# First two gate and up steps on raw x, normalised afterwards, in a spectral-filter and feed-forward kernel

## Chip, cores and metric

The kernel runs on one core of one Trainium2 chip. The metric is the device time of one execution in microseconds. Engines: PE is TensorE (matmuls into PSUM), DVE is VectorE, ACT is ScalarE, POOL is GpSimd, SP is the engine that issues most DMA transfers.

## What is computed

With x of shape (2048, 640) in bf16, and w_gate, w_up (640, 1536), w_down (1536, 640):

```python
xn = (x - mean(x)) / sqrt(var(x) + 1e-5)          # along the 640 columns
s  = irfft2(rfft2(xn) * (w_r + 1j * w_i))         # a two-dimensional spectral filter
h  = gelu(xn @ w_gate) * (xn @ w_up)
g  = silu(h @ w_down)
out = x + s * g
```

## The kernel before, in words

The 2048 rows are sixteen **slabs** of 128 rows, n1 = 0 to 15, four slabs to a **group** (512 rows). A slab goes through these steps:

- Its rows are loaded (`load_x`; DMA issues on SP's queue have line L294) and its mean and 1/sigma are found. `stats` does this on DVE (two `bn_stats` of 320 columns, L393, an aggregate, L396, an add, L397) or on ACT (a pass that sums, L400, then a pass that sums squares, L403), and POOL takes the power -0.5 (L416, L417).
- `apply` (L430, DVE) writes the normalised slab.
- For slabs 0 to 3, `turn_pe` transposes it by five PE transposes (L441) and ACT or DVE copies it to `xnT` (L287, the helper of all PSUM copies). Later slabs are transposed by DMA.
- `fold` (DVE) adds and subtracts mirrored columns, a matmul with the table F1T follows (L497, L498), and the result is stored to DRAM (`D2`) for the spectral part.

The feed-forward part runs beside it. `gate_up(grp, t)` does **step** t of 12 in a group: five matmuls of 512 columns with `Wg` into PSUM tile `pg`, five with `Wu` into `pu` (L840), the gelu on ACT (L852), the product `uT` on DVE (L856). In steps 0 and 1 of group 0 the 512 columns are cut into four pieces of 128, so that each piece needs one slab only. `down` multiplies by `Wd` (L900) and applies the silu; the spectral result multiplies that, x is added, and the output is stored. The spectral part (regrouping loads `BU`, matmuls, products with the filter on DVE, an inverse transform) lies between about 60 and 185 us, interleaved with the feed-forward matmuls of groups 1 to 3.

`pg`, `pu` and `sp` (all other PSUM work) have two buffers each.

The order of the work on every engine is fixed when the program is built. `Plan` holds one task per piece of work, with its engine, an assumed cost, a rank and what it comes after; `Plan.run` fills a simulated clock, always taking the task of lowest rank that is ready. Assumed landing times of transfers come from a model of the wire; after 20 us a task on PE is held back by a margin (2500 ns after a transfer, 250 ns otherwise). On the chip each engine then executes its list in that order, waiting on semaphores.

At the start, x's first slab is loaded in two halves by SP and ACT, a 32 KB identity by POOL, then slabs 1 to 3 and the first weights. Until slab 0 is normalised PE runs `keep_warm` matmuls on a blank tile (L354), sixteen in all, whose results are not used.

Of the kernel before, what the change touches and what calls it, by code (L numbers as in the profile page):

```python
# [15 lines left out]
P = 128  # L16
S = 2048
D = 640
# [96 lines left out]
class Plan:  # L115
# [12 lines left out]
    def add(self, emit, eng, cost, rank, after=(), new=(), use=(), size=0, slow=1.0, hold=0, order=(), lag=0):  # L128
        engs = eng if isinstance(eng, dict) else {eng: cost}
        t = Task(emit=emit, engs=engs, rank=rank, after=list(after), new=list(new), size=size, slow=slow, hold=hold, order=list(order), lag=lag,  # L130
                 seq=len(self.tasks))
        for s in (*new, *use):
            s.users.append(t)
        self.tasks.append(t)
        return t

    def ready(self, t, e, now):
        for a in t.after:
            if a.done is None:
                return None  # L140
        for a in t.order:
            if a.start is None:
                return None
        at = max([0.0] + [a.start + a.engs[e][0] if a.on == e == "PE" else a.done + (0 if a.on == e and not a.size else self.MARGIN[e] + ((2500 if a.size else 250) if e == "PE" and a.start > 20000 else 0)) for a in t.after])
        more = {}
        for s in t.new:
            mine = self.slots[s.tag]
            k = len(mine) - self.bufs[s.tag] + more.get(s.tag, 0)
            more[s.tag] = more.get(s.tag, 0) + 1
            if k >= 0:  # L150
                for u in mine[k].users:
                    if u.done is None:
                        return None
                    at = max(at, u.done + self.MARGIN[e])
        if t.size and e == "SP":
            at = max(at, self.wire - self.BACKLOG)
        return at

    def run(self):
        left, now, order = list(self.tasks), 0.0, []  # L160
        while left:
# [33 lines left out]
            if t.size:  # L195
                self.wire = max(self.wire, now + occ + 900) + t.size * t.slow / 340.0
                t.done = self.wire + (1000 if now < 1000 else 2100 if now < 1700 else 2600 if now < 2700 else 3300 if now < 18000 else 2600 if now < 21000 else 1000) + t.lag
# [22 lines left out]
def kernel(  # L220
# [36 lines left out]
    RSTD = consts.tile([P, NSLAB, 1], FP32)  # L257
    X = persist.tile([P, NSLAB, D], BF16, tag="xb", name="X")
# [5 lines left out]
    D2 = dpool.tile([P, NSLAB, D], BF16)  # L264
    D4 = dpool.tile([NSLAB, 64, 2, LP], BF16)
# [27 lines left out]
    def dma(out, in_, rank, size, after=(), new=(), use=(), slow=1.0, eng=None):  # L293
        return add(lambda e: nc.sync.dma_start(out=out() if callable(out) else out, in_=in_() if callable(in_) else in_),  # L294
                   "SP", (430, 430), rank, after=after, new=new, use=use, size=size, slow=slow)
# [11 lines left out]
    def load_x(a, b):  # L307
        seq[0] += 1
        t = dma(X[:, a:b, :], xv[:, a:b, :], (0, -4, seq[0]), (b - a) * 163840, use=[sX])
        for n in range(a, b):  # L310
            x_in[n] = t
# [8 lines left out]

    def load_gu(a, b):
        cs = slice(a * P, b * P)
        seq[0] += 2
        size = (b - a) * 163840
        i = dma(Wg[:, :, cs], gv[:, :, cs], (0, -4, seq[0] - 1), size, slow=1.1)
        o = dma(Wu[:, :, cs], uv[:, :, cs], (0, -4, seq[0]), size, slow=1.1)
        for t in range(a, b):
            g_in[t], u_in[t] = i, o

    def load_d(h):  # L330
        seq[0] += 1
        t = dma(Wd[:, 6 * h:6 * h + 6, :], dv[:, 6 * h:6 * h + 6, :], (0, -1, seq[0]), 983040)
        for k in range(6 * h, 6 * h + 6):
            d_in[k] = t
# [3 lines left out]
    nc.scalar.dma_start(out=X[64:P, 0, :], in_=xv[64:P, 0, :])  # L338
    nc.scalar.dma_start(out=X[:, 2, :], in_=xv[:, 2, :])
    nc.gpsimd.dma_start(out=ident, in_=tabs["id"])  # L340
# [17 lines left out]
    x_in[0] = dma(X[0:64, 0, :], xv[0:64, 0, :], (0, -4, seq[0]), 163840, use=[sX])  # L358
    load_x(1, 2)
    load_x(3, 4)  # L360
    x_in[2] = tab_in["id"] = x_in[3]
    t = add(blank, "DVE", (330, 400), (0, -9), new=[idle])
    t = keep_warm(8, [t])
    warmed = keep_warm(1, [t, x_in[1]], ns=216)
    load_gu(0, 2)
    load_x(4, 6)
    load_gu(2, 4)
# [9 lines left out]
    load_d(0)  # L377
    load_d(1)
# [5 lines left out]
    def stats(n1, engs):  # L384
        x = X[:, n1, :]
        mean, var, rstd = MVA[:, n1, 0:1], MVA[:, n1, 1:2], RSTD[:, n1, :]
# [12 lines left out]
        def total(e):  # L399
            nc.scalar.activation(out=place(junk, (D,)), in_=x, func=ACT.Copy, scale=-1.0 / D, accum_out=NM[:, n1, :])  # L400

        def square(e):
            nc.scalar.activation(out=junk.tile, in_=x, func=ACT.Square, scale=1.0, bias=NM[:, n1, :], accum_out=var)  # L403
        if eng == "DVE":
            t = add(lambda e: half(e, 0), "DVE", (445, 445), (2, n1), after=after, use=[sX])
            t = add(lambda e: half(e, 1), "DVE", (445, 445), (2, n1), after=[t], use=[sX])
            t = add(moments, "DVE", (345, 450), (2, n1, -1), after=[t])
            if n1 == 0:
                keep_warm(2, [warmed, t], ns=216)
        else:  # L410
            t = add(total, "ACT", (940, 1000), (2, n1), after=after, new=[junk], use=[sX])
            t = add(square, "ACT", (1030, 1100), (2, n1), after=[t], use=[junk, sX])
# [7 lines left out]
        if n1 == 0:  # L420
            keep_warm(1, [warmed, t], ns=216)
        return t, eng

    def apply(n1, root, new):
        sxn, (root, eng) = xn_of[n1 // 2], root

        def go(e):
            if new:
                place(sxn, (2, D))
            nc.vector.tensor_scalar(out=sxn.tile[:, n1 % 2, :], in0=X[:, n1, :],  # L430
                                    scalar1=MVA[:, n1, 0:1] if eng == "DVE" else NM[:, n1, :], scalar2=RSTD[:, n1, :],
                                    op0=ALU.subtract if eng == "DVE" else ALU.add, op1=ALU.mult)
        return add(go, "DVE", (430, 530), (1, n1, 0), hold=250 if n1 < 4 else 0, after=[root], new=[sxn] if new else [], use=[sX] if new else [sX, sxn])

    def turn_pe(n1, ap):
# [6 lines left out]
        a = add(mm, "PE", c_pe(*[140] * 5), (0, n1), after=[ap, tab_in["id"]], new=[pt], use=[sxn])  # L442
        if n1 == 0:
            keep_warm(4, [a], (0, 0, 0), 216)
        turned[n1] = add(lambda e: copy_on(e, xnT[:, :, n1 * P:(n1 + 1) * P], pt.tile),
                         {"DVE": (415, 560)} if n1 == 0 else {"ACT": c_act(640), "DVE": (415, 560)}, None, (0, n1), after=[a], use=[pt], hold=250 if n1 == 0 else 0)
# [61 lines left out]
    lead = ("DVE", "DVE", "ACT", "DVE")  # L508
    for n1 in range(NSLAB):
        if n1 % 2 == 0:  # L510
            xn_of[n1 // 2] = Slot("s1")
        r = stats(n1, (lead[n1] if n1 < 4 else ("ACT" if n1 % 2 else "DVE"),))
# [11 lines left out]


# [302 lines left out]
    def gate_up(grp, t):  # L828
# [3 lines left out]
        for w, ps, wt in ((Wg, pg, g_in[t]), (Wu, pu, u_in[t])):  # L832
            parts = [(128 * j, 128 * j + 128) for j in range(4)] if grp == 0 and t < 2 else [(0, 512)]
            mm = []
            for lo, hi in parts:
                def go(e, w=w, ps=ps, lo=lo, hi=hi):
                    if lo == 0:
                        place(ps, (512,))
                    for c in range(5):
                        nc.tensor.matmul(ps.tile[:, lo:hi], lhsT=w[:, c, t * P:(t + 1) * P],  # L840
                                         rhs=xnT[:, c, grp * 512 + lo:grp * 512 + hi], start=(c == 0), stop=(c == 4),
                                         skip_group_check=True)
                step[0] += 1
                rk = (1, step[0]) if len(parts) == 1 else (1, lo // 128 - 10, t)
                mm.append(add(go, "PE", c_pe(*[hi - lo] * 5), rk,
                              after=[wt] + mm[-1:] + [turned[n] for n in range((grp * 512 + lo) // P, (grp * 512 + hi) // P)],
# [3 lines left out]
        def act(e):  # L850
            place(ge, (512,))
            nc.scalar.activation(out=ge.tile, in_=pg.tile, func=ACT.Gelu_apprx_tanh)  # L852

        def mul(e):
            place(u, (512,))
            nc.vector.tensor_tensor(out=u.tile, in0=pu.tile, in1=ge.tile, op=ALU.mult)  # L856
        a = add(act, "ACT", c_act(512), (0, step[0]), after=[last[id(Wg)]], new=[ge], use=[pg], hold=900 if grp == 0 and t < 2 else 0)
        u_done[grp, t] = add(mul, "DVE", c_dve(512, 1, True), (0, step[0]), after=[a, last[id(Wu)]], new=[u], use=[pu, ge])
# [9 lines left out]
    def down(n1):  # L868
# [6 lines left out]
        done = []  # L875
        parts = ((0, 256, "pg"), (256, 512, "pu"), (512, 640, "pg")) if last else ((0, 320, "pg"), (320, 640, "pu"))
# [16 lines left out]
        for lo, hi, tag in parts:  # L893
            ps, th, mm = Slot(tag), Slot("th"), []
            for k in range(0, 12, 6):
                def go(e, k=k, lo=lo, hi=hi, ps=ps):
                    if k == 0:
                        place(ps, (512,))
                    for t in range(k, k + 6):
                        nc.tensor.matmul(ps.tile[:, 0:hi - lo], lhsT=uT[grp, t].tile[:, j * P:(j + 1) * P], rhs=Wd[:, t, lo:hi],  # L900
                                         start=(t == 0), stop=(t == 11))
                step[0] += 1
                mm.append(add(go, "PE", c_pe(*[hi - lo] * 6), (1, step[0]), new=[] if k else [ps],
                              after=[u_done[grp, t] for t in range(k, k + 6)] + mm + [d_in[k]],
                              use=[uT[grp, t] for t in range(k, k + 6)] + ([ps] if k else [])))
# [73 lines left out]
```

## Time and profile before

| | us |
|---|---|
| median of 10 runs | 203.64 |
| lowest and highest run | 203.43, 204.84 |
| the profiled execution, its own time | 203.41 |
| its span in the profile | 201.6 |
| PE, DVE, ACT busy in the span | 196.2, 146.3, 118.5 |
| mean granted TensorE clock | 0.997 |

The span is what the profile shows from the first to the last instruction. A line of the timeline gives start, duration, engine, source line, operation, output<-input with shape, and count; in brackets stands how long the engine was idle before and what ended the wait. A line of the waits gives the total, how often, and the longest. A line of the chain gives start, duration and what ran; it is followed back from the last instruction.

### The profile page before, as it was taken

What the parts mean: (1) busy time and instruction counts of PE and PEld (TensorE: products, weight loads), DVE (VectorE), ACT (ScalarE), POOL (GpSimd) and SP (SyncE); (2) the same over time, 40 slices, a digit from 0 to 9 for tenths busy, and PEclk for the clock granted to TensorE, in tenths of its full rate; (3) what the DMA queues carried; (4) which work ended last, traced back from release to release, by engine and by line L of the source; (5) the groups of instructions that cost most, each with busy time, mean ns of one, the idle gap of its engine ahead of it and who ended that gap; (6) DMA issues with size and microseconds to landing.
All of it is one profiled execution on the core that took longest, in us unless ns stands there. A gap on an engine that the chain in (4) does not pass through costs nothing.

```text
span 201.6 us, 3986 instructions
## 1 busy us (share of the span) xinstructions
PE 196.2 (97%) x1484; PEld 116.0 (58%) x1484; DVE 146.3 (73%) x321; ACT 118.5 (59%) x204; POOL 27.3 (14%) x60
## 2 busy tenths in 40 slices
PE   7999999999999999999999999999999999999992
PEld 2584444577545455577765454557765555556781
DVE  3798999982322299999999989523277777776774
ACT  2579888445235677687776644513666676666321
POOL 2578333220000000000000000000001111222100
PEclk9999999999999999999999999999999999999998
DMA  5999999899679766514414021069004034444122
GB/s 149 315 325 326 353 375 197 234 235 224 227 251 314 224 139 123 162 56 130 134 44 152 0 68 67 0 194 387 7 3 130 34 98 133 132 130 114 49 68 65
DMA packets 35284, 32.10 MB, mean 159 GB/s; under 512 B 10806, under 2 KB 32306, under 8 KB 35266
## 3 DMA queue, kind: packets, MB, share of 16 engines
q1 hardware_dynamic: 33714, 28.88, 48.8%
q0 software_dynamic: 1184, 2.70, 5.5%
q10 hardware_dynamic: 368, 0.28, 0.5%
q8 instruction: 11, 0.18, 0.4%
q14 instruction: 7, 0.06, 0.1%
HBM read 22.02 MB, written 9.18 MB: 155 GB/s over the span
## 4 chain that ended last, share of the span: by engine, by line
PE 94%; DMA 2%; SPq 1%; ACT 0%; DVE 0%; issue 0%; DVEq 0%
PE pu L840 26%; PE pg L840 26%; PE pg L900 13%; PE pu L900 13%; PE sp L653 3%; PE sp L786 3%; DMA Wu<-in_B_w_up_dram 2%; PE sp L728 2%; PE sp L762 2%; PE sp L626 2%; PE sp L497 2%; SPq L294 1%; PE sp L646 1%; PE sp L780 1%; PE sp L609 0%; PE sp L498 0%
## 5 line engine op out<-in xcount | busy, mean ns | idle before, releaser
L840 PE MATMUL pu<-xnT,Wu 128*128 128x512 bf16 (+1 forms) x270 | 60.7, 355 | 0.1
L840 PE MATMUL pg<-xnT,Wg 128*128 128x512 bf16 (+1 forms) x270 | 60.5, 355 | 0.2 <-ACT xnT L287 0.2
L856 DVE TENSOR_TENSOR uT<-pu,ge 128x512 bf16<-128x512 f32 x48 | 33.0, 689 | 25.9 <-PE pu L840 23.4
L852 ACT ACTIVATE ge<-pg 128x512 bf16<-128x512 f32 x48 | 28.6, 597 | 34.0 <-PE pg L840 33.9
L900 PEld LDWEIGHTS <-uT 128*128 128x128 bf16 x396 | 37.9, 98 | 13.7
L840 PEld LDWEIGHTS <-Wg 128*128 128x128 bf16 x270 | 24.7, 98 | 24.4 <-issue 0.3
L840 PEld LDWEIGHTS <-Wu 128*128 128x128 bf16 x270 | 24.2, 98 | 21.3 <-DMA Wu<-in_B_w_up_dram 0.3
L900 PE MATMUL pg<-Wd,uT 128*128 128x320 bf16 (+2 forms) x204 | 30.5, 293 | 0.0
L900 PE MATMUL pu<-Wd,uT 128*128 128x320 bf16 (+1 forms) x192 | 29.3, 297 | 0.0
L865 POOL DMA_DIRECT2D xr<-in_A_x_dram x16 | 8.7, 544 | 142.3 <-DVE res L888 142.3
L287 ACT CAST ma<-sp 128x644 bf16<-128x644 f32 (+1 forms) x32 | 23.4, 793 | 6.4 <-PE sp L653 4.1
L914 DVE SCALAR_TENSOR_TENSOR G<-th,pg 128x320 bf16<-128x320 f32 (+1 forms) x16 | 7.7, 481 | 9.0 <-ACT th L909 8.9
L909 ACT ACTIVATE th<-pg 128x320 f32<-128x320 f32 (+2 forms) x17 | 7.3, 428 | 11.7 <-PE pg L900 11.5
L914 DVE SCALAR_TENSOR_TENSOR G<-th,pu 128x320 bf16<-128x320 f32 (+1 forms) x16 | 7.7, 482 | 7.9 <-ACT th L909 7.8
L287 ACT CAST mc<-sp 128x640 bf16<-128x640 f32 x16 | 10.6, 692 | 4.2 <-PE sp L498 3.1
L909 ACT ACTIVATE th<-pu 128x320 f32<-128x320 f32 (+1 forms) x16 | 7.0, 437 | 10.4 <-PE pu L900 10.4
L287 ACT CAST Vt<-sp 128x640 bf16<-128x640 f32 x16 | 10.8, 691 | 3.1 <-PE sp L762 3.1
L287 ACT CAST IU<-sp 128x640 bf16<-128x640 f32 x16 | 10.9, 691 | 1.9 <-PE sp L728 1.8
L417 POOL TENSOR_TENSOR RSTD<-MVA,mh 128x1 f32<-128x1 f32 x16 | 9.7, 611 | 13.2 <-DVE MVA L397 12.6
L393 DVE BATCH_NORM_STATS2 STAT<-X 128x6 f32<-128x320 bf16 x18 | 8.7, 486 | 2.8 <-DMA X<-in_A_x_dram 2.8
L287 ACT CAST Z<-sp 128x1024 bf16<-128x1024 f32 x8 | 7.9, 1021 | 1.1 <-PE sp L626 1.1
L706 DVE TENSOR_TENSOR R<-Y 64x644 bf16<-64x644 bf16 x16 | 7.8, 490 | 0.4
(76 smaller groups left out, 210.3 us busy)
## 6 DMA issues: line engine op xcount, KB each, us to landing
BU<-D SPq DMA_DIRECT2D x8, 640.0 KB
D<-mc SPq DMA_DIRECT2D x8, 320.0 KB
xr<-in_A_x_dram POOLq DMA_DIRECT2D x16, 160.0 KB, 3.3
D<-IU SPq DMA_DIRECT2D x8, 320.0 KB
out_dram<-res SPq DMA_DIRECT2D x15, 160.0 KB
Wg<-in_B_w_gate_dram SPq DMA_DIRECT2D x6, 320.0 KB
Wu<-in_B_w_up_dram SPq DMA_DIRECT2D x6, 320.0 KB
Wd<-in_B_w_down_dram SPq DMA_DIRECT2D x2, 960.0 KB
```

Source lines behind the costliest of these rows:

```text
L287: return nc.scalar.copy(out=out, in_=in_) if e == "ACT" else nc.vector.tensor_copy(out=out, in_=in_)
L393: nc.vector.bn_stats(out=STAT[:, n1, 6 * g:6 * g + 6], in_=x[:, 320 * g:320 * g + 320])
L417: nc.gpsimd.tensor_tensor(out=rstd, in0=var, in1=mh, op=ALU.pow)
L653: nc.tensor.matmul(into(q, ri), lhsT=sZ.tile[:, q, ri, :], rhs=FM[:, kinds[q][2] + (4 if ri and kind == 0 else 0), :], start=False, stop=T ...
L706: nc.vector.tensor_tensor(out=o, in0=Yf[:, ::-3, :], in1=Yf[:, 1:3, :], op=ALU.subtract)
L840: nc.tensor.matmul(ps.tile[:, lo:hi], lhsT=w[:, c, t * P:(t + 1) * P], rhs=xnT[:, c, grp * 512 + lo:grp * 512 + hi], start=(c == 0), stop= ...
L852: nc.scalar.activation(out=ge.tile, in_=pg.tile, func=ACT.Gelu_apprx_tanh)
L856: nc.vector.tensor_tensor(out=u.tile, in0=pu.tile, in1=ge.tile, op=ALU.mult)
L865: nc.gpsimd.dma_start(out=sx.tile, in_=xv[:, n1, :])
L900: nc.tensor.matmul(ps.tile[:, 0:hi - lo], lhsT=uT[grp, t].tile[:, j * P:(j + 1) * P], rhs=Wd[:, t, lo:hi], start=(t == 0), stop=(t == 11))
L909: nc.scalar.activation(out=th.tile[:, 0:hi - lo], in_=ps.tile[:, 0:hi - lo], func=ACT.Tanh, scale=0.5)
L914: nc.vector.scalar_tensor_tensor(out=G2.tile[:, lo:hi], in0=th.tile[:, 0:hi - lo], scalar=1.0, in1=ps.tile[:, 0:hi - lo], op0=ALU.add, op1 ...
```

## The change

Step 0 and 1 of group 0 no longer wait for the normalised slabs. Since xn = (x - m) r per row, w'xn = r (w'x - m sum(w)). So the change:

- transposes the raw slabs 0 to 3 on PE (`turn_raw`) and copies them to `XR`; the eight gate and eight up pieces of steps 0 and 1 multiply `XR`;
- sums the columns of the first two Wg and Wu blocks with one-column matmuls against `ones`, copied to `WSUM`;
- writes 1/sigma and -mean of slabs 0 to 3 into `RM`, transposes that on PE (fp32), stores the rows to DRAM (`D5`) and loads them back broadcast to all partitions (`RB`);
- copies the two `pg` and two `pu` tiles of steps 0 and 1 to fp32 tiles, and on DVE adds `RB[1] * WSUM`, multiplies by `RB[0]`, then does the gelu and the product. `down` of group 0 takes steps 0 and 1 last;
- still normalises and transposes slabs 0 to 3, for step 2 on (step 2 is cut into pieces too) and for the spectral part;
- loads x's slab 0 whole on ACT's queue, and on SP's queue first Wg of steps 0 and 1, then slab 1, Wu, slabs 2 and 3; the due times of these are written into the plan (`land`);
- makes the identity (and an fp32 one) on POOL by a memset and a select instead of loading it;
- has seven keep-warm matmuls instead of sixteen;
- moves statistics from DVE to ACT (slabs 6, 10, 14; in the first four slabs 1 and 3 are on ACT instead of slab 2), lowers the assumed ACT cost of them, splits `Wd`'s load 8 and 4 instead of 6 and 6, and lowers the plan's margins after 20 us to 1500 and 150 ns.

The diff, cut to its core:

```diff
-        at = ... ((2500 if a.size else 250) if e == "PE" and a.start > 20000 else 0)) for a in t.after])
+        at = ... ((1500 if a.size else 150) if e == "PE" and a.start > 20000 else 0)) for a in t.after])
...
-    nc.scalar.dma_start(out=X[64:P, 0, :], in_=xv[64:P, 0, :])
-    nc.scalar.dma_start(out=X[:, 2, :], in_=xv[:, 2, :])
-    nc.gpsimd.dma_start(out=ident, in_=tabs["id"])
+    nc.scalar.dma_start(out=X[:, 0, :], in_=xv[:, 0, :])
+    nc.gpsimd.memset(ident, 0.0)
+    nc.gpsimd.affine_select(out=ident, in_=ident, compare_op=ALU.not_equal, fill=1.0, base=0, pattern=[[-1, P]], channel_multiplier=1)
+    nc.gpsimd.memset(ones, 1.0)
...
-    x_in[0] = dma(X[0:64, 0, :], xv[0:64, 0, :], (0, -4, seq[0]), 163840, use=[sX])
-    load_x(1, 2)
-    load_x(3, 4)
-    x_in[2] = tab_in["id"] = x_in[3]
+    x_in[0] = add(lambda e: None, "SP", (1, 1), (0, -5), size=1, land=3550)
+    load_w(Wg, gv, g_in, 0, 2, land=4500)
+    load_x(1, 2, land=4950)
+    load_w(Wu, uv, u_in, 0, 2, land=6150)
+    load_x(2, 3, land=6600)
+    load_x(3, 4, land=7100)
     t = add(blank, "DVE", (330, 400), (0, -9), new=[idle])
-    t = keep_warm(8, [t])
-    warmed = keep_warm(1, [t, x_in[1]], ns=216)
-    load_gu(0, 2)
-    load_x(4, 6)
+    t = warmed = keep_warm(5, [t])
     load_gu(2, 4)
+    load_x(4, 6)
...
-    load_d(0)
-    load_d(1)
+    load_d(0, 8)
+    load_d(8, 12)
...
+    def turn_raw(n1):
+        pt = Slot("sp")
+        def half():
+            return pt.tile[:, 0, :].bitcast(BF16)[:, 0:D]
+        def mm(e):
+            place(pt, (2, 512))
+            for c in range(5):
+                nc.tensor.transpose(out=half()[:, c * P:c * P + P], in_=X[:, n1, c * P:c * P + P], identity=ident)
+        a = add(mm, "PE", c_pe(*[140] * 5), (0, n1), after=[x_in[n1], warmed], new=[pt], use=[sX])
+        if n1 == 0:
+            keep_warm(2, [a], (0, 0, 0))
+        if n1 in (1, 2):
+            k, w, got = ((0, Wg, g_in), (1, Wu, u_in))[n1 - 1]
+            def sums(e, t):
+                for c in range(5):
+                    nc.tensor.matmul(pt.tile[:, 1, 256 + t:257 + t], lhsT=w[:, c, t * P:t * P + P], rhs=ones, start=(c == 0), stop=(c == 4), skip_group_check=True)
...
+        raw[n1] = add(lambda e: copy_on(e, XR[:, :, n1 * P:(n1 + 1) * P], half()...), ...)
...
-    lead = ("DVE", "DVE", "ACT", "DVE")
+    lead = ("DVE", "ACT", "DVE", "ACT")
...
-        r = stats(n1, (lead[n1] if n1 < 4 else ("ACT" if n1 % 2 else "DVE"),))
+        r = stats(n1, (lead[n1] if n1 < 4 else ("ACT" if n1 % 4 else "DVE"),))
...
+    def rows_pe(e):
+        nc.tensor.transpose(out=place(sr, (2, 512))[0:8, 0, 0:P], in_=RM.rearrange("p k n -> p (k n)"), identity=identF)
...
+    rs = dma(D5, lambda: rt.tile[0:8, :], (0, -5, 0), 4096, after=[t], use=[rt])
+    rb_in = dma(RB..., D5.rearrange("k t -> (k t)").partition_broadcast(P), (0, -5, 1), 524288, after=[rs])
...
-            parts = [(128 * j, 128 * j + 128) for j in range(4)] if grp == 0 and t < 2 else [(0, 512)]
+            parts = [(128 * j, 128 * j + 128) for j in range(4)] if grp == 0 and t < 3 else [(0, 512)]
...
+                                         rhs=XR[:, c, lo:hi] if early else xnT[:, c, grp * 512 + lo:grp * 512 + hi], ...
...
+            out = add(lambda e, ev=ev, ps=ps: copy_on(e, place(ev, (512,), FP32), ps.tile), ...)
+            m = add(lambda e, ev=ev, k=k: nc.vector.scalar_tensor_tensor(out=four(ev), in0=RB[:, 1], scalar=WSUM[:, 2 * k + t:2 * k + t + 1], in1=four(ev),
+                                                                         op0=ALU.mult, op1=ALU.add), "DVE", ..., after=[out, rb_in, sums_out[k]], use=[ev])
+            normed.append(add(lambda e, ev=ev: nc.vector.tensor_tensor(out=four(ev), in0=four(ev), in1=RB[:, 0], op=ALU.mult), ...))
...
+        ks = [*range(2, 12), 0, 1] if grp == 0 else [*range(12)]
```

`load_w` is one transfer of a weight block by SP, the half of the former `load_gu`.

In the built order of the changed program, PE's list begins: five keep-warm matmuls; raw transpose of slab 0; two keep-warm; raw transpose of slab 1; gate pieces of slab 0 (steps 0, 1); the ten sums of Wg; up pieces of slab 0; raw transpose of slab 2; five sums of Wu; raw transpose of slab 3; five sums of Wu; the other twelve gate and up pieces with the four normalised transposes between them; step 2 in pieces with the row transpose among them; the first fold matmul after seven of its eight pieces.

## Prediction

> **What bounds the kernel now.** I read the page's shares and slices, TensorE's own waits, the chain that ended last, then the timeline of the first 14 us.
>
> ```profile
> PE 196.2 (97%) x1484; PEld 116.0 (58%) x1484; DVE 146.3 (73%) x321; ACT 118.5 (59%) x204; POOL 27.3 (14%) x60
> PE   7999999999999999999999999999999999999992
> ```
> ```profile
> PE sp L354 <- DVE uT L347: 1.2, 1, 1.2
> PE pg L840 <- ACT xnT L287: 0.2, 1, 0.2
> ```
>
> PE is busy in all slices but the first and the last. Its idle time outside the tail lies before 9.75 us, and there the chain runs over a transfer and a copy:
>
> ```profile
> 3.17 5.02 DMA Wu<-in_B_w_up_dram
> 8.24 0.45 PE pu L840 x5
> 8.69 0.29 PE sp L441 x5
> 9.01 0.70 ACT xnT L287
> 9.75 0.44 PE pg L840 x5
> ```
>
> The timeline shows what PE's "busy" is worth before that:
>
> ```profile
> 1.21 5.12 PE L354 MATMUL sp<-uT 128*128 128x512 bf16 x12 [1.21 <-DVE uT L347]
> 6.17 0.45 PE L441 MATMUL sp<-ident,s 128*128 128x128 bf16 x5
> 6.46 1.03 PE L354 MATMUL sp<-uT 128*128 128x512 bf16 x4
> 7.40 0.72 PE L840 MATMUL pg<-xnT,Wg 128*128 128x128 bf16 x10
> 13.38 0.38 PE L497 MATMUL sp<-mb,F1T 128*128 128x512 bf16 x1
> ```
>
> The sixteen L354 matmuls are warm-up, no result. Five 128-column matmuls (one "piece") start 0.28 us apart from the next five when PE has work (8.53 to 8.81). By 9.75 PE had done seven pieces (three transposes, four gate/up), 1.96 us. Thirteen were left: 9.75 + 13 x 0.28 = 13.39, which is where the first fold matmul starts (13.38). From there PE never waits until the tail. So the end moves by two things only: when the first 13.38 us of work are finished, and any PE wait that is new later.
>
> **What the Trainium skill says here.** TensorE: Matmul & The Clock Gate, What's actually happening: PE runs at 1.2 GHz until a window of about 3.4 us has been busy. The trace agrees in kind: the first twelve warm-ups take 5.12/12 = 0.427 us each, the next four 0.22; full speed came near 6.2 us. Same page, Back-to-back issue gap: start to start does not fall below about 25 ns for small N; the trace has no one-column matmul. DMA: Bandwidth & Descriptors, Anatomy of one DMA: most of the fixed 2 us is the time from the last byte to the signal. Here it was about 1 us (below). VectorE: DVE Perf Modes, The TRN2 errata: an fp32 two-tensor operation of 512 elements takes 691 ns; the trace's uT multiply (L856) takes 689, and the next starts after about 0.61.
>
> **The change part by part.**
>
> *PE work added.* Raw transposes of four slabs: 4 x 0.28 = 1.12 us. Twenty one-column sums with ones: 0.025 each by the page above, 0.056 by the 128-column spacing, so 0.5 to 1.1; I take 0.8, as each still loads 128 weight columns. One fp32 transpose of 8 rows: not in the trace; at least one 0.056 matmul, at most four times that and a latency, 0.1 to 0.4; I take 0.2. Step 2 in four parts: forty at 0.056 for ten at 0.216, +0.1. Sum +2.2 us (1.8 to 2.7) on an engine that is full. Removed: nine of sixteen warm-ups, worth nothing, since they stand in idle time. To break even PE must do 2.2 us more useful work before it turns dense.
>
> *When data lands.* The half-microsecond windows' GB/s sum to 0.21 MB at 3.0 us, 0.45 at 4.0, 0.74 at 5.0, 1.03 at 6.0, 1.35 at 7.0. Wu's last byte (1.35 MB) moved at 7.0 and was seen at 8.24; x0's 0.16 at 2.7, seen at 3.6: 0.9 to 1.2 us late. With Wg first beside x0, the same curve gives Wg 5.1, x1 5.7, Wu 7.0, x2 7.5, x3 8.0. The due times in the diff are 4.5, 4.95, 6.15, 6.6, 7.1. I take the middle: x1 5.3, Wu 6.6, x2 7.05, x3 7.55.
>
> *The new waits of the lead, in the built order.* ScalarE does slab 1's sum (L400's kind: next start 0.72 later) ahead of slab 1's raw copy (about 0.6): 5.3 + 0.72 + 0.6 gives 6.7. The sums of Wg wait for that copy, since they write the same PSUM tile; everything on PE is behind them. Until then PE has only two transposes and two gate pieces to do, which fit even at half clock. Then 0.4 (ten sums), 0.56 (two up pieces), 0.28 (x2), 0.2 (sums of Wu's first), 0.28 (x3): 8.5. The last five sums wait for DVE's raw copy of slab 2, and that stands behind the WSUM copy (needs the Wg sums, done 7.15) and slab 2's two statistics (0.40 apart): 7.55 + 0.8, then the copy to 8.9. PE goes on at about 9.0. Left then: 0.2 of sums, 12 gate/up pieces (3.36), four transposes of the normalised slabs (1.12), the row transpose (0.2): 13.9. Against 13.38 that is +0.5, and with the split step +0.6. With the early and late landings PE goes on at 8.6 or 9.3; with the bounds of the added work the lead is worth -0.2 to +1.3.
>
> *GpSimd.* The identity is now made by a memset and a select instead of a 32 KB load; neither form is in the trace. The library marker that stood before the first power (between 2.1 and 5.0 us) now stands before the select, so 0 to 2.9 us late is possible; the two small selects I put at under 1 us. Even a ready time of 4.6 only delays the first transpose and its copy (to 5.3), and the 6.7 above hides that. No lower end: the old load was not waited for.
>
> *DVE and ScalarE later.* DVE gets eight fp32 passes (8 x 0.61 = 4.9 us) and a 512 copy (0.6), and loses three slabs' statistics (3 x (2 x 0.40 + 0.32) = 3.4). ScalarE gets these (two accumulating passes start 0.72 and 0.82 apart: 3 x 1.54 = 4.6). Counting the built order with such spacings, ScalarE reaches the gelu of step 11 at about 35.6 and DVE its product at about 37, PE needing them at 36.5 and 39: slack of about 1 us each, where the trace had idle gaps of 0.6 to 1.6 before. I take 0.2 for it, 0 to 2.
>
> *The rows' round trip.* The 4 KB store waits in SP's queue for DVE's copy of the rows, about 15.4. Behind it: Wu of steps 8 and 9 (issued at 13.91 now), slabs 12 to 15, the last Wg and Wu, two fold stores, the 0.52 MB broadcast, Wd. Wu is used at 29.6, so its 1.6 us delay is hidden by 10 us of queue; Wd (used at 37.7) likewise. The broadcast lands at about 27 (7.7 MB at 325 GB/s after 2.2 us, and 1 us), and DVE's first use stands at about 28. It costs 1.6 us of wire and nothing, if it is in time. A scratch buffer that ScalarE reuses waits for the store too; that lands about 20, its turn is about 21.
>
> *Reordering by the smaller margins.* The last folds, spectral and inverse work stand some 5 us later on PE. Nothing is added; the last inverse matmul stands 9 us before PE's end instead of 13, and DVE needs about 4 for it. Cost 0 to 0.5, taken as 0.
>
> Sum: +0.6 + 0.2 = **+0.8 us**. Against the profiled execution's 203.41 (span 201.6 and 1.8 around it) that is 204.2; the median of the runs is 0.23 above it, 203.64, so 204.4. Within 0.2%, 0.4 us, a measurement of this kernel cannot tell a change.
>
> **The rivals.**
> - *Faster.* PE is never held by the two copies: the last five sums begin before 8.0 instead of 9.0, and cost 25 ns. For it: the early due times, the idle ScalarE and DVE before 5 us, and a page floor under my 0.04. Against it: DVE's chain alone reaches 8.5 with the earliest landing, and PE is at half clock until about 6.2. The lead becomes 0.6 - 1.0 for the wait - 0.3 for the sums = -0.7, so 202.9. It decides at 8.0.
> - *Break-even.* The sums cost their floor and landings are early: -0.2 to +0.4, so 203.7.
> - *Much slower: the clock.* Only seven warm-ups remain, with gaps; if the window up to 6.2 does not count as busy, PE stays at half speed for 3.4 us more, to 9.6. Its 1.8 us of work before 9.0 doubles, less 0.5 of waits, and 0.3 after: 1.6 on top of the 0.8, so 206.0.
> - *Much slower: the rows come late.* If the broadcast lands at 30 instead of 27, DVE stops 2 us, and with 1 us of slack PE stops 1 or more at the first down products, on top of the 0.8: 205.4.
> - *That nothing of it is done early* is excluded: the built order has the raw pieces ahead of any normalised slab.
>
> **How the numbers follow.** Forecast, +0.4 to +1.6: 0.42. The two slow cases together: 0.24. Break-even: 0.17. Faster: 0.17. So faster 0.17, same 0.17, slower 0.66. The range from 203.0 to 206.6 leaves out about 0.1 on each side.
>
> **What would show it.** The first fold matmul at about 15.9 with seven pieces of step 2 (thirty-five matmuls) ahead of it; sums of Wg starting near 6.7, the last sums near 9.0 with a PE wait on DVE; L354's kind at 0.43 each; no PE wait between 14 and 197. Wrong if PE is dense from before 8, if pieces still start 0.53 apart after 7 us, or if a PE wait appears at 25 to 45 us.

## The result and the profile after

The changed kernel takes 204.52 us (median of 14 runs, 204.15 to 204.91) against 203.82 us for the kernel before beside it (49 runs): a ratio of 1.0033, 95% interval 1.0022 to 1.0044, or 0.67 us slower. The profiled execution took 204.64 us, with a span of 202.6 us, where the kernel before had 203.41 and 201.6.

That pair of profiles shows the kernel before at its best. Of 172 of its executions that ran beside the experiments below, only three have a span as short as 201.6, and their median is 202.1. The changed kernel's fourteen have a median of 202.45, the shortest 202.3. So the spans typically differ by some 0.35 us and not by 1.0. The rest of the loss lies outside the span: the time less the span is 1.77 us in the kernel before and 2.02 in the changed one (medians). What fills this time, no trace shows.

The page's shares, and TensorE's own waits (in the waits: total, how often, longest):

```profile
PE 196.1 (97%) x1546; PEld 118.1 (58%) x1546; DVE 147.6 (73%) x317; ACT 127.6 (63%) x227; POOL 30.9 (15%) x70
```
```profile
PE sp L369 <- DVE uT L362: 1.2, 1, 1.2
PE sp L470 <- DVE XR L297: 0.3, 1, 0.3
PE sp L461 <- DMA X<-in_A_x_dram: 0.3, 1, 0.3
PE sp L470 <- ACT XR L297: 0.2, 1, 0.2
```

PE is as full as before, with 62 more matmuls. Both new waits are at L470, the column sums, and both are for copies of raw slabs (`XR`). The chain of what ended last runs through them:

```profile
1.24 4.08 DMA X<-in_A_x_dram
...
5.35 0.83 ACT th L416 x2
6.18 0.65 ACT XR L297
...
6.87 0.40 PE sp L470 x10
...
7.37 0.16 DVE WSUM L297
7.53 0.79 DVE STAT L409 x2
8.32 0.44 DVE XR L297
...
8.80 0.26 PE sp L470 x5
```

So slab 1's landing, ACT's sum over it, ACT's raw copy, the Wg sums, DVE's copy of them, two statistics, DVE's raw copy, the last sums: the order and nearly the times of the prediction (sums at 6.7 and 9.0). The timeline of PE adds what the pieces cost, and where the dense part begins:

```profile
6.87 0.39 PE L470 MATMUL sp<-ones,Wg 128*128 128x1 bf16 x10 [0.19 <-ACT XR L297]
7.12 0.72 PE L891 MATMUL pu<-XR,Wu 128*128 128x128 bf16 x10
...
8.80 0.26 PE L470 MATMUL sp<-ones,Wu 128*128 128x1 bf16 x5 [0.28 <-DVE XR L297]
8.93 0.72 PE L891 MATMUL pg<-XR,Wg 128*128 128x128 bf16 x10
...
13.95 0.27 PE L570 MATMUL sp<-identF,RM 128*8 128x128 f32 x1
14.06 0.72 PE L891 MATMUL pg<-xnT,Wg 128*128 128x128 bf16 x10
...
15.45 0.38 PE L538 MATMUL sp<-mb,F1T 128*128 128x512 bf16 x1
```

Starts are what counts here: ten sums from 6.87 to 7.12, 25 ns each; the row transpose from 13.95 to 14.06, 0.11. The first fold matmul is at 15.45, with seven pieces of step 2 (1.96 us) ahead of it that the kernel before did later: 13.49 against 13.38. In this pair the lead costs 0.11 us. It varies from execution to execution: e11 below, with the same order on PE as the kernel before, has its first fold matmul at 13.97, and e9, with the same as the changed kernel, at 15.21. The rest of the pair's difference is elsewhere, and the timeline's end shows most of it. Before:

```profile
196.90 0.83 PE L900 MATMUL pg<-Wd,uT 128*128 128x128 bf16 x12
...
198.08 0.29 DVE L918 TENSOR_TENSOR mc<-s,pg 128x128 f32<-128x128 bf16 x1
...
199.14 0.36 ACTq L930 DMA_DIRECT2D out_dram<-res  x1
```

And after:

```profile
core 0 of [0], span 202.6 us
...
197.20 0.83 PE L968 MATMUL pg<-Wd,uT 128*128 128x128 bf16 x12
...
198.38 0.29 DVE L986 TENSOR_TENSOR mc<-s,pg 128x128 f32<-128x128 bf16 x1
198.58 0.28 DVE L956 TENSOR_TENSOR res<-yg,xr 128x256 bf16<-128x256 bf16 x1
...
199.64 0.35 ACTq L998 DMA_DIRECT2D out_dram<-res  x1
```

The span's +1.0 us splits into three: PE's last block starts 0.30 later; from there to the last store's issue it takes 2.44 us and not 2.24, because a 256-column residual sum (L956) now stands between `mc` and the rest on DVE; and from that issue to the end of the span it takes 2.96 and not 2.46. The table has these numbers from every kernel run here (us; one profiled execution each, whose span is printed to 0.1). Its last two columns are medians over all executions of the kernel, those of the kernel before over the 172:

| kernel | first fold matmul | PE's last block | last block to last issue | last issue to end | span | median span | time less span |
|---|---|---|---|---|---|---|---|
| before | 13.38 | 196.90 | 2.24 | 2.46 | 201.6 | 202.1 | 1.77 |
| after | 15.45 | 197.20 | 2.44 | 2.96 | 202.6 | 202.45 | 2.02 |
| e1 residual reads eased | 15.29 | 196.94 | 2.33 | 2.83 | 202.1 | 202.3 | 2.05 |
| e2 without raw x | 15.41 | 199.01 | 2.24 | 2.55 | 203.8 | 203.7 | 1.80 |
| e3 sums left out | 14.21 | 195.96 | 2.44 | 2.90 | 201.3 | 201.5 | 1.85 |
| e4 sums late | 14.58 | 196.53 | 2.24 | 2.93 | 201.7 | 201.6 | 1.85 |
| e5 before, new loads | 13.53 | 197.33 | 2.24 | 2.53 | 202.1 | 202.1 | 1.79 |
| e6 before, small margins | 13.40 | 198.44 | 2.24 | 2.52 | 203.2 | 202.9 | 1.85 |
| e7 sums late, margins 1000/100 | 14.75 | 196.38 | 2.24 | 2.98 | 201.6 | 201.65 | 1.84 |
| e8 sums late, one keep-warm | 15.28 | 196.91 | 2.24 | 2.95 | 202.1 | 202.5 | 1.86 |
| e9 after, one Wd load | 15.21 | 197.03 | 2.44 | 2.53 | 202.0 | 202.1 | 2.04 |
| e10 sums late, one Wd load | 15.35 | 196.98 | 2.24 | 2.48 | 201.7 | 201.4 | 1.98 |
| e11 before, three Wd loads | 13.97 | 197.49 | 2.24 | 2.97 | 202.7 | 202.55 | 1.84 |
| e12 e10, correction left out | 15.82 | 196.10 | 2.24 | 2.56 | 200.9 | 201.0 | 1.78 |

The second column compares only kernels with the same work ahead of the first fold matmul. The kernels with raw x have seven pieces of step 2 there, 0.28 us each; e3 has eight, and e12 eight and five 512-column matmuls of step 3 (1.08 us). Those without raw x have none, and e5 has one piece of step 1 fewer.

An estimate of where PE's last block starts in a typical execution is the median span less the two stretches behind that block. It gives 197.4 for the kernel before (e11: 197.3), 197.05 for the changed kernel (e9: 197.1) and 196.4 for e4. By this estimate the change gains about 0.3 us up to PE's last block, and loses some 0.65 between there and the end of the span and 0.25 outside it.

### The profile page after: what moved, and what is told of

The parts are those of the page before. It is cut to its first block, busy times and chain, and to the rows that moved or that the text cites. A ratio compares the mean times of both kernels' runs of the same rounds, so it can differ in the third digit from the quotient of the medians.

```text
span 202.6 us, 4147 instructions
## 1 busy us (share of the span) xinstructions
PE 196.1 (97%) x1546; PEld 118.1 (58%) x1546; DVE 147.6 (73%) x317; ACT 127.6 (63%) x227; POOL 30.9 (15%) x70
## 4 chain that ended last, share of the span: by engine, by line
PE 94%; DMA 2%; DVE 1%; ACT 1%; issue 0%; SPq 0%; DVEq 0%
PE pg L891 25%; PE pu L891 25%; PE pg L968 13%; PE pu L968 13%; PE sp L703 3%; PE sp L836 3%; PE sp L778 2%; PE sp L812 2%; DMA X<-in_A_x_dram 2%; PE sp L676 2%; PE sp L538 2%; PE sp L696 1%; PE sp L830 1%; PE sp L484 1%; PE sp L539 0%; PE sp L659 0%
## 5 line engine op out<-in xcount | busy, mean ns | idle before, releaser
L891 PE MATMUL pu<-xnT,Wu 128*128 128x512 bf16 (+1 forms) x245 | 57.3, 366 | 0.0
L891 PE MATMUL pg<-xnT,Wg 128*128 128x512 bf16 (+1 forms) x245 | 57.3, 366 | 0.0
L908 DVE TENSOR_TENSOR uT<-pu,ge 128x512 bf16<-128x512 f32 x46 | 31.7, 690 | 26.6 <-PE pu L891 22.8
L904 ACT ACTIVATE ge<-pg 128x512 bf16<-128x512 f32 x46 | 27.6, 600 | 30.2 <-PE pg L891 29.9
L891 PEld LDWEIGHTS <-Wg 128*128 128x128 bf16 x285 | 25.4, 98 | 23.3
L891 PEld LDWEIGHTS <-Wu 128*128 128x128 bf16 x285 | 24.9, 98 | 21.0
L431 POOL TENSOR_TENSOR RSTD<-MVA,mh 128x1 f32<-128x1 f32 x12 | 8.2, 686 | 0.8
L416 ACT ACTIVATE th<-X 128x640 bf16<-128x640 bf16 x11 | 8.1, 734 | 0.1
L756 DVE TENSOR_TENSOR R<-Y 64x644 bf16<-64x644 bf16 x16 | 7.8, 490 | 0.4
L758 DVE TENSOR_TENSOR R<-Y 64x644 bf16<-64x644 bf16 x16 | 7.8, 486 | 0.3
```

The lines of the kernel that those rows point to most:

```text
L431: nc.gpsimd.tensor_tensor(out=rstd, in0=var, in1=mh, op=ALU.pow)
L756: nc.vector.tensor_tensor(out=o, in0=Yf[:, ::-3, :], in1=Yf[:, 1:3, :], op=ALU.subtract)
L758: nc.vector.tensor_tensor(out=o, in0=Y[:, 0], in1=Y[:, 1], op=ALU.add)
L904: nc.scalar.activation(out=ge.tile, in_=pg.tile if src is None else src, func=ACT.Gelu_apprx_tanh)
L908: nc.vector.tensor_tensor(out=u.tile, in0=pu.tile if src is None else src, in1=ge.tile, op=ALU.mult)
```

## The experiments

### What in the lead costs: e3 and e4

e3 leaves the sums out, and what uses them no longer waits for them:

```diff
-        if n1 in (1, 2):
+        if n1 in ():
...
+    nc.gpsimd.memset(WSUM, 0.0)
```

> The changed kernel with the twenty one-column matmuls and the two copies of their sums left out (the correction of the mean is computed with a zero in place of the column sums). Measured on the profile after: 20 x 25 ns of matmuls = 0.5 us, and two waits of 0.2 and 0.3 us before them on TensorE. Theory A: the first fold matmul at about 14.5 to 15.0 rather than 15.45, the time 0.4 to 1.0 us below the changed kernel, ratio 0.9985 to 1.0015. Rival D (the lead has slack: later stages wait for DMA and engines anyway): within 0.2 us of the changed kernel.

Measured: 203.44 us, ratio 0.9967 (0.9953 to 0.9982). e4 keeps all twenty sums and moves them behind the row transpose, into its PSUM tile:

```diff
-        if n1 in (1, 2):
+        if n1 in ():
...
+    ss = [add(lambda e, k=k, w=w, t=t: col_sums(k, w, t), "PE", (132, 370), (0, 7, k, t), after=[got[t], rows_done], use=[sr])
+          for k, (w, got) in enumerate(((Wg, g_in), (Wu, u_in))) for t in range(2)]
+    both = add(lambda e: copy_on(e, WSUM, sr.tile[:, 1, 256:260]), ..., (0, 9), after=ss, use=[sr])
```

> The changed kernel with the twenty column-sum matmuls moved out of the two early slots to just after the transpose of the rows, in that transpose's own PSUM tile, with one copy of four columns. No TensorE work is taken away, only the two waits of 0.2 and 0.3 us ahead of the sums and the hold on the PSUM slot. Theory A: 0.2 to 0.6 us below the changed kernel, ratio 1.000 to 1.0025. Rival D (waits ahead of the sums only moved idle time that would lie at the next load anyway): within 0.1 us, ratio 1.003.

Measured: 203.48 us, ratio 0.9971 (0.9955 to 0.9987). Rival D falls, and theory A was too small: with twenty tiny matmuls in another place the change turns from a loss into a gain of 0.3%. Not all of that is due to the waits in the lead. DVE's order at the end changed with it, and the way from PE's last block to the last issue is 2.24 us again, 0.2 less. In the lead itself, e4's first fold matmul comes 0.63 us before that of e9, which has the early sums and also had the full clock by 5.2 us (below). e3 is no faster than e4 by the times, although it lacks the sums' 0.5 us of work: PE's last block comes 0.57 us earlier in its profile, about 0.3 by the estimate from the median spans, and 0.2 of that goes to the worse end on DVE. The timeline of e4:

```profile
5.48 0.72 PE L898 MATMUL pg<-XR,Wg 128*128 128x128 bf16 x10
6.42 0.73 PE L898 MATMUL pu<-XR,Wu 128*128 128x128 bf16 x10 [0.23 <-DMA Wu<-in_B_w_up_dram]
6.99 0.44 PE L461 MATMUL sp<-ident,X 128*128 128x128 bf16 x5
```

From 6.42 on PE runs piece after piece, where the changed kernel waited for ScalarE until 6.87 and for DVE until 8.80. The sums write the second bank of a two-bank tile whose first bank the raw copy reads, and the wait is for the copy all the same. The Trainium skill (PSUM — Partial Sum Buffer, PSUM bank collisions raise a hardware error) says that two engines on different banks do not collide; no run here takes that wait away by itself, so this stays its word.

### The end on VectorE: e1

```diff
-        xr_in[n1] = sx, add(go, "POOL", (600, 600), (5, n1), after=[y_done[n1]], ...)
+        xr_in[n1] = sx, add(go, "POOL", (600, 600), (5, n1), after=[y_done[min(n1, 12)]], ...)
```

> The changed kernel with one dependency eased: the residual reads of the last three slabs no longer wait for that slab's inverse stage. TensorE, ScalarE, GpSimd and SyncE keep their orders instruction for instruction; only VectorE's last ten instructions stand differently (the 640-wide residual sum of slab 14 ahead of slab 15's first gate product). Theory A (about half of the +0.67 us is a tail in which VectorE's late sums push the last store back by 0.2 us and bunch the output stores): 0.2 to 0.6 us below the changed kernel, ratio to the kernel before 1.000 to 1.0025; TensorE's last block still starts at about 197.2. Rival B (the whole loss is made on TensorE by the added matmuls, the tail is incidental): within 0.1 us of the changed kernel, ratio 1.003.

Measured: 204.28 us, ratio 1.0006 (0.9992 to 1.0020). That is in theory A's band and below rival B's 1.003, but the gain over the changed kernel compares two intervals that almost touch. The trace confirms only part: last block to last issue went from 2.44 to 2.33, and the median span is 0.15 shorter. The other 0.39 of e1's shorter span lies in PE's last block, 0.26, whose order wasn't touched, and after the last issue, 0.13.

### After the last issue: e7, and then e9 to e11

I first took the extra 0.5 us after the last issue for stores and loads that a late inverse stage bunches at the end. e7 puts that stage twelve matmuls earlier:

```diff
-   ... ((1500 if a.size else 150) if e == "PE" and a.start > 20000 else 0)) for a in t.after])
+   ... ((1000 if a.size else 100) if e == "PE" and a.start > 20000 else 0)) for a in t.after])
```

> The kernel with the late sums, with slack 1000/100 for 1500/150: the last inverse stage then stands 12 matmuls (1.6 us) earlier, and TensorE's work is the same. Theory A (a late last inverse bunches loads and stores at the end: the end comes 2.9 us after the last issue rather than 2.5 as before): 0.1 to 0.4 us below the kernel with the late sums, ratio 0.995 to 0.997. Rival F (the 0.4 us after the last issue has another cause): the same ratio as the late sums within 0.001, and the end still 2.8 to 3.0 us after the last issue.

Measured: 203.47 us, ratio 0.9980 (0.9969 to 0.9992), the end 2.98 after the issue. Theory A falls. The table then showed a pattern: 2.83 to 2.98 in six kernels, 2.46 to 2.55 in four. In the built programs the six have their last store signal the first of eight DMA semaphores, which are dealt out in turn (DMAHW0), the others the seventh or eighth (DMAHW6, DMAHW7). And SyncE's list ends with waits for DMAHW0, 1, 2 up to 7, in this order. One transfer more or less, far from the end, moves the last store on by one. e9 is the changed kernel with that, e10 the late sums with it, and e11 gives the kernel before the same fault:

```diff
# e9, e10
-    load_d(0, 8)
-    load_d(8, 12)
+    load_d(0, 12)
# e11
-    load_d(0)
-    load_d(1)
+    load_d(0, 6), load_d(6, 9)
+    load_d(9, 12)
```

> The changed kernel with Wd loaded in one transfer rather than two: one transfer less before the end, so that the last store signals the eighth of the eight DMA semaphores (DMAHW7) and not the first (DMAHW0). The closing sequence on SyncE waits for the eight in order; a first one that comes last leaves seven more waits to step through. TensorE, ScalarE and GpSimd keep their orders, VectorE too. Theory H (the 0.4 us that the end comes later after the last issue in the changed kernel is this): span end minus last issue 2.5 rather than 2.96, ratio 1.0005 to 1.002. Rival J (it is something in the raw-x path itself): 2.8 to 3.0, ratio 1.0025 to 1.004.

> The kernel with the late column sums, and Wd in one transfer, so that its last store too signals DMAHW7. Theory H: 0.4 us below the late sums alone, ratio 0.994 to 0.9965, span end minus last issue 2.5. Rival J: the same as the late sums, ratio 0.997 to 0.9985.

> The kernel before with Wd in three transfers rather than two: one more transfer, so that its last store signals DMAHW0. All other orders are as in the kernel before. Theory H: 0.4 us slower, ratio 1.001 to 1.003, span end minus last issue 2.9 to 3.0. Rival J: ratio 0.999 to 1.001, 2.45 to 2.55.

Measured: e9 204.12 us, ratio 1.0019 (1.0005 to 1.0034); e10 203.42 us, 0.9969 (0.9954 to 0.9985); e11 204.40 us, 1.0023 (1.0011 to 1.0035). The timelines' ends, e9 and e11:

```profile
core 0 of [0], span 202.0 us
...
199.47 0.35 ACTq L998 DMA_DIRECT2D out_dram<-res  x1
```
```profile
core 0 of [0], span 202.7 us
...
199.73 0.35 ACTq L930 DMA_DIRECT2D out_dram<-res  x1
```

The changed kernel's end now takes 2.53 us, that of the kernel before 2.97: rival J falls, and theory H holds in all fourteen rows of the table. The waits themselves can be seen on SyncE: how many there are, their shortest, median and longest in ns, and when the first and the last start. In the changed kernel, after the last store has landed:

```profile
L1042 SPq EVENT_SEMAPHORE  x8: 27/28/28, 201.3 to 201.7; - x8
```

And in e9, before the last stores have landed, and then:

```profile
L1042 SPq EVENT_SEMAPHORE  x6: 28/28/28, 199.7 to 200.0; - x6
L1042 SPq EVENT_SEMAPHORE  x3: 28/28/28, 200.3 to 201.1; - x3
```

The changed kernel steps through all eight at the end, about 0.06 us apart; e9 has most of them behind it by then. The seven that are left when the first is the last to come are worth 0.4 to 0.5 us. By the times alone only e11 is clear: e9's interval overlaps that of the changed kernel, and e10's ratio lies just outside its expected band and equals e4's. The median spans show it in all three: 0.45 us longer in e11 than in the kernel before, 0.35 shorter in e9 than in the changed kernel, 0.2 shorter in e10 than in e4. In e10 the time outside the span is 0.13 longer than in e4 and hides most of that; why it is longer stays open.

### The clock: e8

```diff
-    t = warmed = keep_warm(5, [t])
+    t = warmed = keep_warm(1, [t])
```

> The kernel with the late sums, with one keep-warm matmul in place of five ahead of the first transpose (the two after it stay). The prediction held open that the clock stays low until 9.6 us and costs 1.6 us. Theory A (the clock rises after some 4 us of work on TensorE, whatever the work is; without the first four matmuls it rises about 1.7 us later, at about 7 to 8.5 us, and what runs until then at half speed costs 0.5 to 1.2 us): ratio 0.9995 to 1.003. Rival G (the clock follows time since the start, or transposes and small matmuls lift it as well): within 0.2 us of the late sums, ratio 0.996 to 0.998.

Measured: 204.40 us, ratio 1.0022 (1.0009 to 1.0035), 0.9 us above e4. PE's timeline:

```profile
3.60 0.71 PE L461 MATMUL sp<-ident,X 128*128 128x128 bf16 x5 [1.78 <-DMA X<-in_A_x_dram]
...
5.65 1.27 PE L898 MATMUL pg<-XR,Wg 128*128 128x128 bf16 x10
6.72 1.13 PE L898 MATMUL pu<-XR,Wu 128*128 128x128 bf16 x10
7.69 0.44 PE L461 MATMUL sp<-ident,X 128*128 128x128 bf16 x5
```

The gate pieces start 1.07 apart for ten matmuls, twice the usual 0.56; full speed comes at about 7.6 us. Theory A holds: four keep-warm matmuls in idle time are worth about 0.9 us here (median spans 202.5 and 201.6), as useful work now stands where the kernel before had only warm-up. Whether the kind of work matters to the clock wasn't tested.

The same thing moves without any edit, so a single profile couldn't tell e8 from e4; the 22 executions of each do. e4 and e10 have the same order on PE, but in the profile of e10 the gate pieces are the cold ones again:

```profile
5.84 1.27 PE L898 MATMUL pg<-XR,Wg 128*128 128x128 bf16 x10
6.91 1.02 PE L898 MATMUL pu<-XR,Wu 128*128 128x128 bf16 x10
```

Full speed came by about 5.2 us in e4, 6.3 in e7 and 7.2 in e10, with the first fold matmul at 14.58, 14.75 and 15.35. The Trainium skill (TensorE: Matmul & The Clock Gate, What's actually happening) says that the activity window runs freely and that the point of release therefore differs from run to run, by about half a microsecond each way; in these three it differs too, but over 2 us, and that the window runs freely stays the page's word. In the changed kernel it mattered less: with the early sums in place PE waited for the two copies anyway (first fold 15.21 with the clock full by 5.2, 15.45 by 6.2).

### The other parts: e2, e5, e6, e12

e2, the changed kernel without raw x, in short:

```diff
-        early = grp == 0 and t < 2
+        early = False
...
-    t = warmed = keep_warm(5, [t])
+    t = warmed = keep_warm(12, [t])
```

> The changed kernel without its main idea: load order, identity built on GpSimd, the split of the statistics and the smaller margins stay, but the first two steps multiply normalised x as before (no transposes of raw x, no column sums, no rows, no broadcast, keep-warm set back to 12). Theory A (raw x buys about 1.5 us of earlier start and pays about 2.2 us of added matmuls and gaps, so it is worth nothing or less): 203.2 to 204.2 us, ratio 0.997 to 1.002, first fold matmul between 12.5 and 14.0. Rival C (the earlier loads are worthless without raw x, which carries a gain that the tail hides): 205 us or more, first fold matmul later than 14.5.

Measured: 205.53 us, ratio 1.0075 (1.0048 to 1.0102). The number is rival C's, the cause is neither. PE stood idle for DVE's copy and ran cold after it:

```profile
8.49 0.50 PE L880 MATMUL pg<-xnT,Wg 128*128 128x128 bf16 x5 [1.81 <-DVE xnT L297]
...
9.32 0.74 PE L482 MATMUL sp<-ident,s 128*128 128x128 bf16 x5
```

From 9.32 (0.74 long) pieces start 0.53 apart where 0.28 is usual. So I put the load order into the kernel before, which has its keep-warm matmuls in place:

```diff
# on the kernel before: x0 whole on ScalarE, identity by memset and select, and on SyncE
+    load_w(Wg, gv, g_in, 0, 2, land=4500)
+    load_x(1, 2, land=4950)
+    load_w(Wu, uv, u_in, 0, 2, land=6150)
+    load_x(2, 3, land=6600)
+    load_x(3, 4, land=7100)
```

> The kernel before with the changed kernel's load order alone (x0 whole as one load on ScalarE's queue, Wg, x1, Wu, x2, x3 in a row on SyncE's; identity built on GpSimd); the first steps still use normalised x. Theory A (the load order costs the normalised path and only pays with raw x, because x1 to x3 now come after weights that the first gate needs a normalised slab for): first gate at 7.5 to 8.3 rather than 7.40, first fold matmul at 13.8 to 15.0 rather than 13.38, time 204.3 to 205.5 us, ratio 1.002 to 1.008. Rival B2 (the load order is neutral and the +1.7 us of the kernel without raw x came from TensorE's clock being cold after a 1.8 us gap that was left without keep-warm matmuls): ratio 0.999 to 1.001.

Measured: 203.91 us, ratio 0.9995 (0.9981 to 1.0008). Theory A falls: the load order alone is neutral. e2's loss came from the gap and the low clock after it: by its profile the first fold matmul is 2.03 us later than in the kernel before, and the way from there to PE's last block takes 183.60 us, where it took 183.52.

e6 gives the kernel before the smaller margins, 1500 and 150 for 2500 and 250.

> The kernel before with the smaller slack in the order alone (1500/150 for 2500/250). Theory A (the slack reorders the middle and the end without a stall on TensorE): ratio 0.998 to 1.001, because the last inverse stage still lies ahead of the last gate and up steps and VectorE's last twelve instructions keep their order. Rival E (the smaller slack costs waits on TensorE after 20 us, and is part of the changed kernel's loss): ratio 1.001 to 1.004, with waits of TensorE on ScalarE or VectorE that the kernel before does not have.

Measured: 204.72 us, ratio 1.0038 (1.0019 to 1.0056). Rival E holds for that kernel, whose times spread from 203.46 to 206.53. Behind the lead PE gained three waits, at folds and in the spectral part:

```profile
PE sp L728 <- DVE R L708: 0.5, 1, 0.5
PE sp L497 <- ACT mc L287: 0.3, 1, 0.3
PE sp L728 <- DVE R L706: 0.2, 1, 0.2
```

The changed kernel, with the same margins, has none of these, so this isn't part of its loss as the profile shows it; its own order with the old margins wasn't run.

e12 is e10 with the correction of steps 0 and 1 left out:

```diff
+        a = add(act, "ACT", c_act(512), (0, 100), after=[last[id(Wg)]], new=[ge], use=[pg])
+        u_done[grp, t] = add(mul, "DVE", c_dve(512, 1, True), (0, 100), after=[a, last[id(Wu)]], new=[u], use=[pu, ge])
+        return
         normed, evs = [], []
```

> The kernel with late sums and one Wd transfer, with the correction of steps 0 and 1 left out: gelu and product read the raw-x PSUM tiles as they are (four fp32 copies and eight fp32 passes less; the broadcast rows are still loaded, nobody reads them). The prediction put 0.2 us, 0 to 2, on this added work of VectorE and ScalarE. Theory A (TensorE never waits for it, so it is hidden): the same ratio as with it within 0.0015. Rival K (VectorE at 9 tenths between 20 and 40 us delays evictions that TensorE or the stores need): 0.3 to 1 us faster.

Measured: 202.74 us, ratio 0.9953 (0.9934 to 0.9972) against e10's 0.9969. The difference of 0.0016 lies between the two expectations, and the intervals overlap. The traces say more. e12 does one piece of step 2 (0.28 us) and a block of step 3 (1.08) ahead of its first fold matmul that e10 does behind it:

```profile
14.74 1.24 PE L898 MATMUL pg<-xnT,Wg 128*128 128x512 bf16 x5
15.82 0.38 PE L538 MATMUL sp<-mb,F1T 128*128 128x512 bf16 x1
```

With these two counted, it is 181.64 us from the first fold matmul to PE's last block in e12 and 181.63 in e10. So in these executions PE loses nothing to the correction, as in theory A. e12's last block comes 0.88 us before e10's because its first 13 us went faster: its clock was full by about 5.2, e10's by 7.2. Of the 0.68 us between the two median times, 0.2 lies outside the span; how much of the rest is the clock's chance, in nine executions against 22, stays open.

## Why the prediction was right, and where it wasn't

The forecast was 204.4 us and slower at 0.66; it came out at 204.52, slower by 0.67 us where 0.8 was forecast. The direction and the total hold, the terms don't: that their errors nearly cancelled is luck.

- **Path and times of the lead: right.** Sums of Wg at 6.7, in the trace 6.87; last sums at 9.0, in the trace 8.80 (8.64 in e1, 8.56 in e9), behind the waits and the queue on DVE that were named. The 2 us that the prediction quotes as a transfer's fixed cost are given there for transfers that GpSimd issues; these were issued by SyncE and ScalarE, and the prediction rightly used the 0.9 to 1.2 us of its own trace.
- **Size of the lead: +0.6 predicted (0.5 of it up to the first fold matmul), +0.11 measured in the pair.** First fold at 15.9, in the trace 15.45. The last sums started 0.2 earlier; a sum costs 25 ns where I took 40, which saves 0.07 on the last five; the row transpose takes 0.11 where I took 0.2. The page's floor that I had named was the right price. And the 13.38 that all this was set against comes from an execution faster than nearly all others; e11 gets there at 13.97. So the lead probably gains in a typical execution: the estimate has the change 0.3 us ahead at PE's last block, where it was to be 0.8 behind.
- **Later: +0.2 predicted, +0.19 measured in the pair,** only in part where I put it. From the first fold matmul to PE's last block it is 181.75 us, and before 183.52; less the seven pieces' 1.96 that is +0.19. Of this 0.08 is step 2 cut into pieces, which I had counted in the lead. Another 0.09 is a wait of the fold at 25.5 for DVE; e1, with the same order on PE, doesn't have it, and e9 has 0.16. The gelu of step 11 starts at 36.49, not at 35.6, without a gap on PE. ScalarE's busy time rose by 9.1 us (118.5 to 127.6), twice the 4.6 counted for the moved statistics, and PE didn't notice.
- **The rows: right.** DVE's first pass over `RB` starts at 27.9, as predicted (28), and waits for nothing:

```profile
27.86 0.75 DVE L921 SCALAR_TENSOR_TENSOR IU<-RB,WSUM,IU 128x512 f32<-128x512 f32 x1
```

- **Reordering and the end: 0 predicted, about 0.65 measured.** This step failed. The 0 to 0.5 looked for a late inverse stage. What came is 0.2 from one residual sum ahead of the last products, and about 0.45 from the last store's semaphore. Neither is in a busy time or a wait of PE; both are in the built order, and in no view that I had read. Neither came with the smaller margins alone (e6: 2.24 and 2.52).
- **Time outside the span: put at the 1.8 us of the kernel before, measured 2.02.** The sum had no term for a change of it. Its cause stays open.
- **The clock rival: not in the profile after,** where full speed came at about 6.2; but e8 and e10 show that the risk was real, and e8 its price, about 0.9 us.
- **"Faster", with PE not held by the two copies: right as a mechanism.** e4 gets there by moving the sums, not by earlier landings, and gives 203.48.

So +0.8 was forecast ahead of the end, where the estimate gives -0.3; the 0.65 at the end and the 0.25 outside the span, both put at nothing, made up for it. The version to keep is e4 or e10: 0.9971 and 0.9969 of the kernel before.

## What to carry to other kernels

When work is moved ahead of a full engine, ask of each small helper when it is needed: the column sums were needed at 28 us and stood at 7, in a tile whose other half was being read. Before two profiles are subtracted, set each span beside those of other executions of the same kernel: here the pair differed by 1.0 us, the medians by 0.35. Split a difference at the end of a trace into the engine's last block, the way from there to the last issue, and the way from the issue to the end; the last part can change by which semaphore the last transfer happens to signal. And work that moves into the first 7 us runs at whatever clock the engine has then.

## What was not expected of the hardware

- Seven waits in a closing sequence, all long fulfilled, took about 0.06 us each: from the last issue to the end it is 2.46 to 2.56 us with the last store on DMAHW6 or 7, and 2.83 to 2.98 with it on DMAHW0.
- A one-column matmul with 128 weight columns starts 25 ns after the one before it, weight load included (ten in 0.25 us). The Trainium skill (TensorE: Matmul & The Clock Gate, Back-to-back issue gap) has that floor; the trace agrees.
- A 128x128 select on GpSimd takes 0.29 us, a memset of that size 0.21: the identity was ready at 1.5 us, where slab 0 was seen at 3.76.
